# A half step of four rows of 256 tokens on 128 partitions in place of two rows of 480 on 64, in a fused attention and feed-forward kernel

## The chip, the cores and the metric

The kernel runs on one core of one Trainium2 chip. The metric is the device time of one execution in microseconds. The core has a matrix engine (PE, with its weight loads shown apart as PEld), a vector engine (DVE), an activation engine (ACT), a general engine (POOL) and a sync engine (SP), which here issues every transfer between the chip's main memory and the on-chip memory of 128 partitions. Each engine works through its own instructions in program order and waits on semaphores for the others.

## What is computed

Four batches of 12,480 tokens with 128 channels are reduced to 32 summary rows each by attention (the 32 `inducing` rows ask, all tokens answer), and then every token attends to the 32 rows of its batch. The result goes through a feed-forward network of 2,048 units with the nonlinearity h - tanh(h).

```python
B, N, m, C = 4, 12480, 32, 128
scale = 1.0 / np.sqrt(C)
def mab(q, kv):
    s = scale * (q @ kv.transpose(0, 2, 1))
    s = s - s.max(-1, keepdims=True)
    a = np.exp(s)
    a /= a.sum(-1, keepdims=True) + 1e-09
    return a @ kv
h = mab(I, x)                      # I: inducing, for each batch
x = mab(x, h).reshape(B * N, C)    # every token over 32 rows
g = x @ w_in                       # 128 -> 2048
return (g - np.tanh(g)) @ w_out    # 2048 -> 128
```

## The kernel before

The kernel never forms the 2,048 units of each token. A token's attention result is a weighted mean of the 32 rows of its batch, so the feed-forward network is expanded around the mean of those rows: `linear` makes one 32x128 matrix per batch (kept four times over the partitions as `P4`), which takes a token's 32 attention weights to its output. A bound (`bound`) is computed beside it; if it were exceeded, a general path behind a branch would run. On these inputs it does not.

A batch is cut into steps of 1,920 tokens (`SG`): four rows (`NQ`) of 480 tokens (`SEG`), one row for each group of 32 partitions, so that a step's scores for 32 queries fill 128 partitions by 480. 12,480 tokens are six such steps and a half step of 960 tokens. In the kernel before, the half step has two rows of 480 and fills 64 partitions. `SGS` lists the steps.

The first half of a batch (`first`, which calls `attend` for one or two groups of steps): for each step, SP loads `xT` (channels on partitions, L347); PE makes the scores against the 32 inducing rows (L332) into a bank of PSUM; DVE copies them to `s1` and takes the maximum (L358). When a group's maximum is known (`nb`), ACT takes the exponential (L408), DVE transposes blocks of 32x32 (`et`, L412), and PE sums the weighted tokens into `bank` (L419), 15 column steps of 32 tokens per row. For that it needs the tokens on partitions (`xn`): either SP loads them from a second copy in memory (L401, `in_xn`, or `in_xl` for the half step), or, for the steps listed in `TURNED`, PE transposes `xT` (L391) and ACT copies the result (L397). From the sums comes the batch's `hT` (L478 on PE, L480 on DVE), and from that `linear`.

The second half (`second`, `b_chain`): PE makes each step's scores against `hT` (L332 again), DVE transposes (`be`, L604) and takes maxima (L606), POOL subtracts (L611), ACT takes the exponential (L613), POOL folds 32 columns to 16 (L618), DVE sums and inverts (L621, L624), POOL scales (L625), DVE transposes back (`bt`, L628), PE multiplies by `P4` (`o`, L653), ACT copies `o` out of PSUM to `ot` (L659; in the last batch DVE may take it too, and the target is a free `xT` buffer), and SP stores it (L663). Stores hold 960 tokens each.

The two weight matrices arrive as 64-bit floats and are taken apart to 32-bit on DVE, ACT and POOL (`weight`, L283 to L308), through buffers of the `xn` pool.

The order is planned while the program is built. Every piece of work is entered with `add`: engine, planned cost, buffers read and written, a priority. `Plan.order` plays the plan through: whenever an engine is free it starts the ready piece with the lowest priority number, provided that the pools still have buffers (`PLACES`, for example ten `xT`, five `xn`, six `ot`, three PSUM banks `ps`). The numbers of `ORD` shift the priorities by batch and kind. The instructions are then issued in that order, on each engine's queue, and stay in it. Where the plan sees PE idle, matmuls on `ident` without use are put in (L744), in the share `FILL` of the gap.

```python
SGS = [(s * SG, NQ) for s in range(NS)] + ([(NS * SG, QL)] if QL else [])
...
add("SP", nq * 0.6, lambda x=x, s=s, P=P: nc.sync.dma_start(
    out=x.get()[:P], in_=xn[b, :, s * KB:(s + 1) * KB, :] if s < NS else xl[b]),
...
for _ in range(int(FILL * gaps.get(op, 0.0) / 0.25)):
    nc.tensor.matmul(bank[:, 2 * C:2 * C + 128], lhsT=ident, rhs=ident, start=first_fill, stop=True,
```

Of the kernel before, what the change touches and what calls it, by code (L numbers as in the profile page):

```python
# [30 lines left out]
ORD = dict(first=(-155, 195, 380, 915), second=(430, 815, 820, 935), fs=(16, 24, 10, 6), ss=(56, 54, 79, 44),  # L31
           lx=(-251, -205, -237, -234), ln=(-61, -146, -54, -80), lns=(8, 1, 49, 8), turn=(59, 65, 77, 55),
           keep=(-35, -146, -86, -29), q=(-534, -529, -468, -487), half=(-225, -211, -158, -86),
           late=(220, 276, 264, 244), guard=1420, win=-237, wout=-113, lwin=-162.5, lwout=291.5,
           store=(-272, -267, -265, -343), base=(43, 109, 36, 51))
# [150 lines left out]
def fused_kernel(ctx, tc, xT, xn, xl, indT, w_in, w_out, outT):  # L186
    nc = tc.nc
    C, NTOK = xT.shape
    B = xn.shape[0]
    m = indT.shape[1]  # L190
# [4 lines left out]
    QL = (N - NS * SG) // SEG  # L195
    SGS = [(s * SG, NQ) for s in range(NS)] + ([(NS * SG, QL)] if QL else [])
# [132 lines left out]
    def scores(ps, rows, w):  # L329

        for q, row in enumerate(rows):
            nc.tensor.matmul(ps[q * m:(q + 1) * m, :SEG], lhsT=w, rhs=row, start=True, stop=True)  # L332

    def attend(b, pri, s1, group, nbs, sms, at, hacc):
# [9 lines left out]
        for s in group:  # L344
            base, nq = SGS[s]
            x = xT_b[b, s] = io_buf("xT", [C, SG])
            add("SP", nq * 0.6, lambda x=x, base=base, nq=nq: nc.sync.dma_start(  # L347
                out=x.get()[:, :nq * SEG], in_=xT[:, b * N + base:b * N + base + nq * SEG]),
                writes=[x], pri=pri + s - of("lx", b), lag=IN_LAG, turn="xT")
            ps = misc()  # L350

            def pe(x=x, ps=ps, nq=nq):
                t = x.get()[:, :nq * SEG].rearrange("c (k q j) -> c k q j", k=KB, j=32)
                scores(ps.get(), [t[:, :, q, :] for q in range(nq)], indT_sb)
            add("PE", 0.96, pe, reads=[x, ind_b, s1], writes=[ps], pri=pri + of("fs", b) * s)
# [4 lines left out]
            add("DVE", 0.68, out, reads=[ps, s1], writes=[s1_part[s], mxg], pri=pri + of("fs", b) * s)  # L360
# [18 lines left out]
        for s in group:  # L379
            base, nq = SGS[s]  # L380
            P = nq * m
            x = io_buf("xn", [128, KB, C])
            parts = []
            if (b, s) in TURNED and nq == NQ:
                for k in range(0, KB, NT):
                    n = min(NT, KB - k)
# [13 lines left out]
            else:  # L400
                add("SP", nq * 0.6, lambda x=x, s=s, P=P: nc.sync.dma_start(  # L401
                    out=x.get()[:P], in_=xn[b, :, s * KB:(s + 1) * KB, :] if s < NS else xl[b]),
                    writes=[x], pri=p + of("lns", b) * s - of("ln", b), lag=IN_LAG, turn="xn")
            q0 = p + of("q", b) + of("fs", b) * s

            def ex(s=s, P=P):
                sl = s1.get()[:P, s, :]
                nc.scalar.activation(out=sl, in_=sl, func=AF.Exp, scale=SC, bias=nb.get()[:P],  # L408
                                     accum_out=sums.get()[:P, s:s + 1])
            add("ACT", 0.88, ex, reads=[nb, s1], writes=[s1_part[s], sums], pri=q0)  # L410
            et = io_buf("et", [128, KB, m])
            add("DVE", 0.66, lambda et=et, s=s, P=P: nc.vector.transpose(  # L412
                out=et.get()[:P].rearrange("p k i -> p (k i)"), in_=s1.get()[:P, s, :]),
                reads=[s1_part[s], s1], writes=[et], pri=q0)

            def acc(et=et, x=x, s=s, P=P):
                for k in range(KB):
                    q = k % NQ
                    nc.tensor.matmul(hacc.get()[q * m:(q + 1) * m, :], lhsT=et.get()[:P, k, :], rhs=x.get()[:P, k, :],  # L419
                                     start=(s == group[0] and k < NQ), stop=(s == group[-1] and k >= KB - NQ))  # L420
            last = add("PE", 1.03, acc, reads=[et, x, *parts], writes=[hacc], pri=q0)
# [166 lines left out]
    def b_chain(b, nq, x, xs, pri, S, out, roomy):  # L588
        P = nq * m
        ps = misc()  # L590
        add("PE", 0.96, lambda: scores(ps.get(), [xs()[:, q * SEG:(q + 1) * SEG] for q in range(nq)], hTs[b]),
# [12 lines left out]
        add("DVE", 0.68, lambda: nc.vector.transpose(out=be.get()[:P].rearrange("p k i -> p (k i)"), in_=ps.get()[:P, :SEG]),  # L604
            reads=[ps, *held], writes=[be], pri=pri)
        add("DVE", 0.64, lambda: nc.vector.tensor_reduce(out=bmx.get()[:P], in_=be.get()[:P], axis=AX.X, op=ALU.max),  # L606
            reads=[be], writes=[bmx], pri=pri)

        def wide(t):
            return t.unsqueeze(2).to_broadcast([P, KB, m])  # L610
        add("POOL", 1.02, lambda: nc.gpsimd.tensor_tensor(out=be.get()[:P], in0=be.get()[:P], in1=wide(bmx.get()[:P]), op=ALU.subtract),  # L611
            reads=[bmx], writes=[be], pri=pri)
        add("ACT", 0.6, lambda: nc.scalar.activation(out=be.get()[:P], in_=be.get()[:P], func=AF.Exp, scale=SC),  # L613
# [4 lines left out]
        add("POOL", 0.7, lambda: nc.gpsimd.tensor_tensor(out=bs.get()[:P, :, :m // 2], in0=be.get()[:P, :, :m // 2],  # L618
                                                         in1=be.get()[:P, :, m // 2:], op=ALU.add),
            reads=[be], writes=[bs], pri=pri)  # L620
        add("DVE", 0.42, lambda: nc.vector.tensor_reduce(out=S()[:P], in_=bs.get()[:P], axis=AX.X, op=ALU.add),  # L621
            reads=[bs], writes=[part], pri=pri)
        s_parts.append(part)
        add("DVE", 0.24, lambda: nc.vector.reciprocal(out=brs.get()[:P], in_=S()[:P]), reads=[part], writes=[brs], pri=pri)  # L624
        add("POOL", 1.02, lambda: nc.gpsimd.tensor_tensor(out=be.get()[:P], in0=be.get()[:P], in1=wide(brs.get()[:P]), op=ALU.mult),  # L625
            reads=[brs], writes=[be], pri=pri)

        add("DVE", 0.67, lambda: nc.vector.transpose(out=bt.get()[:P], in_=be.get()[:P].rearrange("p k i -> p (k i)")),  # L628
# [3 lines left out]
    def second(b, s, pri):  # L632
        base, nq = SGS[s]
        x = xT_b[b, s]
        n = (b * NSG + s) * KB

        def out(bt, held):
            ots = []
            for h in range(nq // 2):
                if b < B - 1:  # L640
                    ots.append(io_buf("ot", [128, 2 * SEG]))
                else:
                    if h == 0:

                        wide = io_buf("xT", [C, SG])
                    ots.append(Buf(lambda wide=wide, h=h: wide.get()[:, 2 * h * SEG:2 * (h + 1) * SEG]))
            keep = [wide] if b == B - 1 else []
            tiles = [Buf(lambda: ps_o.tile([128, 2, 512], F32, name="o"), "o") for _ in range(nq // 2)]

            def pe(qs):  # L650
                for q in qs:
                    p = slice(q * m, (q + 1) * m)
                    nc.tensor.matmul(tiles[q // 2].get()[:, q % 2, :SEG], lhsT=P4_b[b].get()[p, :], rhs=bt.get()[p, :],  # L653
                                     start=True, stop=True)

            add("PE", 1.05, lambda: pe(range(nq)), reads=[bt, *held, P4_b[b]], writes=tiles, pri=pri)
            for h, (o, ot) in enumerate(zip(tiles, ots)):
                def ev(copy, o=o, ot=ot):
                    copy(out=ot.get().rearrange("p (q n) -> p q n", q=2), in_=o.get()[:, :, :SEG])  # L659
                add("ACT", 0.97, lambda ev=ev: ev(nc.scalar.copy), reads=[o, *keep], writes=[ot], pri=pri,  # L660
                    other=("DVE", 1.14, lambda ev=ev: ev(nc.vector.tensor_copy), pri + 1000) if b == B - 1 else None)
                at = b * N + base + 2 * h * SEG
                add("SP", 1.2, lambda ot=ot, at=at: nc.sync.dma_start(out=outT[:, at:at + 2 * SEG], in_=ot.get()),  # L663
                    reads=[ot, *keep], pri=pri - of("store", b), lag=OUT_LAG)
        b_chain(b, nq, x, x.get, pri, lambda: sums_all.get()[:, n:n + KB], out, b == B - 1 and s % 2 == 1)


# [190 lines left out]
```

## Time and profile before

| | us |
|---|---|
| Three runs, median (lowest to highest) | 216.4 (213.31 to 217.84) |
| Profiled execution | 213.38 |
| Its span, first to last instruction | 211.8 |
| PE busy in it | 177.3 |
| DVE busy | 150.5 |
| ACT busy | 118.1 |
| POOL busy | 96.6 |

The profile is of one execution. Busy times overlap; a stage is limited by whatever ends last in it. The page cuts the span into 40 slices of 5.3 us and gives the busy tenths of each engine, the PE clock that was granted, the share of time in which the 16 transfer engines had packets, and the rate in GB/s. The lines that carry the argument stand in the prediction.

### The profile page before, as it was taken

How to read it: one execution, taken by the hardware profiler on the slowest of the kernel's cores; microseconds unless marked ns; L12 is line 12 of the kernel's file. 1: busy time of each engine (PE TensorE's matmuls, PEld its weight loads, DVE VectorE, ACT ScalarE, POOL GpSimd, SP SyncE). 2: the span in 40 equal slices, each digit the busy share in tenths (PEclk: the TensorE clock that was granted, in tenths of full speed). 3: DMA queues.
4: the chain of work that ended last, by engine and by line, in shares of the span. 5: the costliest groups of instructions: out<-in, count | busy, mean ns of one | idle time of the engine just before them, and what ended most of it. 6: DMA issues, size and time to landing. Idle time of an engine off the chain costs nothing.

```text
span 211.8 us, 5313 instructions
## 1 busy us (share of the span) xinstructions
PE 177.3 (84%) x2055; PEld 96.6 (46%) x2055; DVE 150.5 (71%) x392; ACT 118.1 (56%) x230; POOL 96.6 (46%) x138
## 2 busy tenths in 40 slices
PE   7589988489897896999699499986999699899950
PEld 7544566353352365542225366431556334346620
DVE  5798469519997975479679637896688227997970
ACT  2446658313323876577549457553997456566530
POOL 1044003201599543148846306597427224989610
PEclk9969999958999999999999979999999959999995
DMA  5999999999799999999999999999999991548791
GB/s 169 414 425 422 406 387 373 199 410 371 245 413 429 361 351 292 424 405 422 425 409 400 345 367 395 356 331 376 429 403 310 408 415 73 204 161 354 305 398 75
DMA packets 15468, 73.40 MB, mean 346 GB/s; under 512 B 1872, under 2 KB 1872, under 8 KB 15440
## 3 DMA queue, kind: packets, MB, share of 16 engines
q1 hardware_dynamic: 15440, 73.03, 90.2%
q8 instruction: 17, 0.28, 0.5%
q14 instruction: 11, 0.09, 0.1%
HBM read 47.46 MB, written 25.56 MB: 345 GB/s over the span
## 4 chain that ended last, share of the span: by engine, by line
PE 41%; DMA 38%; DVE 7%; ACT 5%; issue 3%; SPq 2%; POOL 1%; ACTq 0%; DVEq 0%; POOLq 0%
DMA xT<-in_xT 22%; PE ps_m L332 11%; PE o L653 10%; PE bank L419 5%; PE ps_m L391 5%; DMA xn<-in_xl 5%; PE bank L744 4%; DMA xn<-in_xn 4%; DMA xn<-in_w_out 4%; DMA outT<-ot 4%; PE ps_m L501 2%; ACT ot L659 2%; PE ps_m L513 2%; ACT s L408 1%; PE ps_m L459 1%
## 5 line engine op out<-in xcount | busy, mean ns | idle before, releaser
L659 ACT COPY ot<-o 128x960 f32<-128x960 f32 x39 | 36.5, 957 | 13.2 <-PE o L653 7.2
L419 PE MATMUL bank<-xn,et 128*32 128x128 f32 (+1 forms) x840 | 32.0, 285 | 7.7 <-DMA xn<-in_xn 3.4
L332 PE MATMUL ps_m<-xT,indT_sb 128*32 128x480 f32 x208 | 29.9, 625 | 9.4 <-DMA xT<-in_xT 7.3
L611 POOL TENSOR_TENSOR be<-be,bmx 128x480 f32<-128x480 f32 (+1 forms) x25 | 25.6, 1028 | 17.6 <-DVE bmx L606 16.5
L625 POOL TENSOR_TENSOR be<-be,brs 128x480 f32<-128x480 f32 (+1 forms) x25 | 24.7, 993 | 17.3 <-DVE brs L624 12.5
L419 PEld LDWEIGHTS bank<-xn,et 128*32 128x32 f32 (+1 forms) x840 | 24.9, 113 | 15.4 <-issue 6.0
L653 PE MATMUL o<-bt,P 32*128 32x480 f32 x184 | 29.6, 623 | 1.1 <-ACT ot L659 1.0
L332 PE MATMUL ps_m<-xT,hT_all 128*32 128x480 f32 x208 | 27.4, 586 | 0.7 <-DVE be L604 0.5
L618 POOL TENSOR_TENSOR bs<-be 128x240 f32<-128x240 f32 (+1 forms) x25 | 17.4, 697 | 22.3 <-ACT be L613 17.7
L397 ACT COPY xn<-ps_m 128x512 f32<-128x512 f32 (+1 forms) x32 | 17.1, 560 | 16.1 <-PE ps_m L391 16.1
L358 DVE TENSOR_SCALAR_CACHE_REDUCE s<-ps_m 128x480 f32<-128x480 f32 (+1 forms) x28 | 18.1, 645 | 10.3 <-PE ps_m L332 10.2
L744 PE MATMUL bank<-ident 128*128 128x128 f32 x150 | 23.3, 303 | 1.4 <-POOL ident masks.py:199 1.4
L744 PEld LDWEIGHTS bank<-ident 128*128 128x128 f32 x150 | 20.4, 211 | 6.2 <-issue 4.8
L391 PE MATMUL ps_m<-ident,xT 128*128 128x128 f32 x120 | 18.8, 299 | 4.3 <-DMA xT<-in_xT 3.7
L408 ACT ACTIVATE s<-s,nb 128x480 f32<-128x480 f32 (+1 forms) x28 | 19.5, 697 | 3.2 <-DVE nb L377 3.2
L391 PEld LDWEIGHTS ps_m<-ident,xT 128*128 128x128 f32 x120 | 14.3, 151 | 12.9 <-issue 3.6
L613 ACT ACTIVATE be<-be 128x480 f32<-128x480 f32 (+1 forms) x25 | 14.9, 606 | 8.8 <-POOL be L611 8.8
L412 DVE STREAM_TRANSPOSE et<-s 128x480 f32<-128x480 f32 (+1 forms) x28 | 17.9, 651 | 2.5 <-ACT s L408 2.4
L308 POOL TENSOR_TENSOR wout_sb<-wout_sb,xn 128x512 f32<-128x512 f32 x4 | 5.6, 1398 | 30.5 <-DVE xn L304 26.6
L628 DVE STREAM_TRANSPOSE bt<-be 128x480 f32<-128x480 f32 (+1 forms) x25 | 16.4, 657 | 4.0 <-POOL be L625 3.8
L604 DVE STREAM_TRANSPOSE be<-ps_m 128x480 f32<-128x480 f32 (+1 forms) x25 | 16.3, 660 | 3.8 <-PE ps_m L332 3.8
L606 DVE TENSOR_REDUCE bmx<-be 128x15 f32<-128x480 f32 (+1 forms) x25 | 15.5, 621 | 0.1
(126 smaller groups left out, 223.6 us busy)
## 6 DMA issues: line engine op xcount, KB each, us to landing
xT<-in_xT SPq DMA_DIRECT2D x24, 960.0 KB, 8.8
outT<-ot SPq DMA_DIRECT2D x39, 480.0 KB, 8.2
xn<-in_xn SPq DMA_DIRECT2D x16, 960.0 KB, 9.4
outT<-xT SPq DMA_DIRECT2D x13, 480.0 KB, 2.9
xn<-in_w_in SPq DMA_DIRECT2D x4, 512.0 KB, 5.4
xn<-in_w_out SPq DMA_DIRECT2D x4, 512.0 KB, 8.4
xT<-in_xT SPq DMA_DIRECT2D x4, 480.0 KB, 8.8
xn<-in_xl SPq DMA_DIRECT2D x4, 480.0 KB, 9.1
```

The source lines that it names most:

```text
L332: nc.tensor.matmul(ps[q * m:(q + 1) * m, :SEG], lhsT=w, rhs=row, start=True, stop=True)
L358: nc.vector.tensor_scalar(out=s1.get()[:P, s, :], in0=ps.get()[:P, :SEG], scalar1=1.0, scalar2=None, op0=ALU.mult, op1=ALU.max, accum_out= ...
L391: nc.tensor.transpose(out=pt.get()[:, i * 128:(i + 1) * 128], in_=xT_b[b, s].get()[:, (k + i) * 128:(k + i + 1) * 128], identity=ident)
L408: nc.scalar.activation(out=sl, in_=sl, func=AF.Exp, scale=SC, bias=nb.get()[:P], accum_out=sums.get()[:P, s:s + 1])
L412: add("DVE", 0.66, lambda et=et, s=s, P=P: nc.vector.transpose(out=et.get()[:P].rearrange("p k i -> p (k i)"), in_=s1.get()[:P, s, :]), re ...
L419: nc.tensor.matmul(hacc.get()[q * m:(q + 1) * m, :], lhsT=et.get()[:P, k, :], rhs=x.get()[:P, k, :], start=(s == group[0] and k < NQ), sto ...
L611: add("POOL", 1.02, lambda: nc.gpsimd.tensor_tensor(out=be.get()[:P], in0=be.get()[:P], in1=wide(bmx.get()[:P]), op=ALU.subtract), reads=[ ...
L618: add("POOL", 0.7, lambda: nc.gpsimd.tensor_tensor(out=bs.get()[:P, :, :m // 2], in0=be.get()[:P, :, :m // 2], in1=be.get()[:P, :, m // 2: ...
L625: add("POOL", 1.02, lambda: nc.gpsimd.tensor_tensor(out=be.get()[:P], in0=be.get()[:P], in1=wide(brs.get()[:P]), op=ALU.mult), reads=[brs] ...
L653: nc.tensor.matmul(tiles[q // 2].get()[:, q % 2, :SEG], lhsT=P4_b[b].get()[p, :], rhs=bt.get()[p, :], start=True, stop=True)
L659: copy(out=ot.get().rearrange("p (q n) -> p q n", q=2), in_=o.get()[:, :, :SEG])
L744: nc.tensor.matmul(bank[:, 2 * C:2 * C + 128], lhsT=ident, rhs=ident, start=first_fill, stop=True, skip_group_check=not first_fill)
```

## The change

The half step is laid out as four rows of 256 tokens on 128 partitions (`HEG`), 1,024 tokens in all. A batch has only 960 left, so the half step begins 64 tokens (`DUP`) earlier and repeats the last 64 of the step before. In the first half of the attention the repeated tokens must not count twice: their scores (64 partitions by 32 columns) are set to -3.0e38 after the maximum is taken. In the second half their outputs are computed and not stored: the half step's two copies go side by side into one `ot` buffer, and one store takes the 960 tokens behind the repeated ones. The column steps of L419 become 8 for 15 in the half step, the loads of it 128 partitions by 4 KB for 64 by 7.5 KB (`xl`) and 4 KB for 3.75 KB a partition (`xT`).

Pools change (`xT` 11 for 10, `bt` 2 for 5, `et` 4 for 3, `ot` 5 for 6 and larger), `ORD`, `FILL` and the lag that the plan takes for loads (`IN_LAG`) get new numbers, and `TURNED` has nine steps for eight.

```diff
+HEG = 256
+HB = HEG // 32
+DUP = NQ * HEG - SG // 2
-FILL = 0.7
-PLACES = dict(xT=10, xn=5, s1=1, be=5, bt=5, et=3, ot=6, ps=3, o=2, bs=1, D=1, M4=1, P1=2, P4=2)
+FILL = 0.8
+PLACES = dict(xT=11, xn=5, s1=1, be=5, bt=2, et=4, ot=5, ps=3, o=2, bs=1, D=1, M4=1, P1=2, P4=2)
-ORD = dict(first=(-155, 195, 380, 915), second=(430, 815, 820, 935), fs=(16, 24, 10, 6), ss=(56, 54, 79, 44),
+ORD = dict(first=(-205, 200, 455, 875), second=(435, 945, 825, 1020), fs=(16, 32, 18, 9), ss=(21, 111, 96, 66),
...
-TURNED = {(0, 0), (0, 2), (0, 3), (0, 4), (2, 0), (2, 1), (3, 0), (3, 3)}
+TURNED = {(0, 0), (0, 1), (0, 2), (0, 3), (0, 5), (2, 0), (2, 4), (3, 0), (3, 5)}
-IN_LAG, OUT_LAG = 2.5, 1.7
+IN_LAG, OUT_LAG = 2, 1.7
...
-    SGS = [(s * SG, NQ) for s in range(NS)] + ([(NS * SG, QL)] if QL else [])
+    SGS = [(s * SG, SEG, 0) for s in range(NS)] + ([(NS * SG - DUP, HEG, DUP)] if N > NS * SG else [])
...
+    def share(us, seg):
+        return us if seg == SEG else 0.15 + (us - 0.15) * seg / SEG
...
-            def out(ps=ps, s=s, P=nq * m):
-                nc.vector.tensor_scalar(out=s1.get()[:P, s, :], in0=ps.get()[:P, :SEG], scalar1=1.0, scalar2=None,
-                                        op0=ALU.mult, op1=ALU.max, accum_out=mxg.get()[:P, s:s + 1])
+            def out(ps=ps, s=s, seg=seg, dup=dup):
+                nc.vector.tensor_scalar(out=s1.get()[:, s, :seg], in0=ps.get()[:, :seg], scalar1=1.0, scalar2=None,
+                                        op0=ALU.mult, op1=ALU.max, accum_out=mxg.get()[:, s:s + 1])
+                if dup:
+
+                    nc.vector.memset(s1.get()[:dup, s, :32], -3.0e38)
...
-                add("SP", nq * 0.6, lambda x=x, s=s, P=P: nc.sync.dma_start(
-                    out=x.get()[:P], in_=xn[b, :, s * KB:(s + 1) * KB, :] if s < NS else xl[b]),
+                add("SP", NQ * seg / 800.0, lambda x=x, s=s, kb=kb: nc.sync.dma_start(
+                    out=x.get()[:, :kb], in_=xn[b, :, s * KB:(s + 1) * KB, :] if s < NS else xl[b]),
...
+            elif full:
+                ots, keep = [io_buf("ot", [128, NQ * HEG]) for _ in range(2)], []
+            else:
+                whole = io_buf("ot", [128, NQ * HEG])
+                ots = [Buf(lambda h=h: whole.get()[:, 2 * h * seg:2 * (h + 1) * seg]) for h in range(2)]
+                keep = [whole]
...
+            if not full:
+                at = b * N + base
+                add("SP", 1.2, lambda: nc.sync.dma_start(out=outT[:, at + dup:at + NQ * seg], in_=whole.get()[:, dup:NQ * seg]),
+                    reads=[whole, *ots], pri=pri - of("store", b), lag=OUT_LAG)
```

What this moves is shown at three places. The first is SP's queue from batch 0's loads to the first loads `xn` of batch 1. `xT` and `xn` are the token loads, `in_xl` the half step's rows, `in_w_out` the second weight matrix. Before:

```order
L347 DMA xT<-in_xT 128x1920 x6
L401 DMA xn<-in_xn 128x1920
L347 DMA xT<-in_xT 128x960
L283 DMA xn<-in_w_out 128x1024
L347 DMA xT<-in_xT 128x1920
L283 DMA xn<-in_w_out 128x1024
L347 DMA xT<-in_xT 128x1920
L401 DMA xn<-in_xn 128x1920
L401 DMA xn<-in_xl 64x1920
L347 DMA xT<-in_xT 128x1920
L283 DMA xn<-in_w_out 128x1024 x2
L401 DMA xn<-in_xn 128x1920 x4
```

Now, on the same queue:

```order
L354 DMA xT<-in_xT 128x1920 x6
L354 DMA xT<-in_xT 128x1024
L287 DMA xn<-in_w_out 128x1024 x2
L354 DMA xT<-in_xT 128x1920 x2
L411 DMA xn<-in_xn 128x1920
L287 DMA xn<-in_w_out 128x1024
L354 DMA xT<-in_xT 128x1920 x2
L411 DMA xn<-in_xl 128x1024
L287 DMA xn<-in_w_out 128x1024
L411 DMA xn<-in_xn 128x1920 x4
```

Batch 0 loads one `xn` where it loaded two, four loads `xT` of batch 1 stand ahead of the wait for free buffers where three stood, and `xl` stands behind them on 128 partitions.

The second place is PE, from the last batch's sums (`bank`) to its `linear` (`win_sb`). `P_1287` and `P_1826` are the matrices `P4` of batches 1 and 2, `fold,P` makes `hT`. Before:

```order
L653 MATMUL o<-bt,P_1287 128x480 x4
L419 MATMUL bank<-xn,et 32x128 x15
L459 MATMUL ps_m<-sm,fold 128x1
L419 MATMUL bank<-xn,et 32x128 x15
L653 MATMUL o<-bt,P_1826 128x480 x4
L478 MATMUL ps_m<-fold,P_2154 128x32
L744 MATMUL bank<-ident 128x128 x2
L501 MATMUL ps_m<-win_sb,hT_all 32x512 x4
```

Now, with `P_1857` for batch 2:

```order
L667 MATMUL o<-bt,P_1857 128x480 x4
L428 MATMUL bank<-xn,et 32x128 x15
L763 MATMUL bank<-ident 128x128
L428 MATMUL bank<-xn,et 32x128 x30
L468 MATMUL ps_m<-sm,fold 128x1
L667 MATMUL o<-bt,P_1857 128x480 x4
L428 MATMUL bank<-xn,et 32x128 x8
L763 MATMUL bank<-ident 128x128 x2
L487 MATMUL ps_m<-fold,P_2164 128x32
L667 MATMUL o<-bt,P_1857 128x480 x4
L510 MATMUL ps_m<-win_sb,hT_all 32x512 x4
```

An output matmul of batch 2 still stands ahead of the matmul for `hT`, now ahead of the half step's sums too, and fillers stand between.

The third place is PE in the tail, from the second scores of the last batch to its first output. `P_2326` is batch 3's matrix. Before:

```order
L653 MATMUL o<-bt,P_1826 128x480 x4
L332 MATMUL ps_m<-xT,hT_all 32x480 x12
L653 MATMUL o<-bt,P_1826 128x480 x2
L555 MATMUL ps_m<-wout_sb,M_2189 32x128 x16
L332 MATMUL ps_m<-xT,hT_all 32x480 x4
L559 MATMUL ps_m<-P_2306,fold 128x128
L332 MATMUL ps_m<-xT,hT_all 32x480 x2
L653 MATMUL o<-bt,P_2326 128x480 x4
```

Now, where `P_1239` is batch 1's matrix and `P_2347` batch 3's:

```order
L667 MATMUL o<-bt,P_1857 128x480 x4
L339 MATMUL ps_m<-xT,hT_all 32x480 x12
L763 MATMUL bank<-ident 128x128 x2
L564 MATMUL ps_m<-wout_sb,M_2201 32x128 x16
L667 MATMUL o<-bt,P_1857 128x256 x4
L568 MATMUL ps_m<-P_2323,fold 128x128
L339 MATMUL ps_m<-xT,hT_all 32x480 x4
L667 MATMUL o<-bt,P_1239 128x256 x4
L339 MATMUL ps_m<-xT,hT_all 32x256 x4
L701 MATMUL ps_m<-xT,cols 32x128 x16
L667 MATMUL o<-bt,P_2347 128x480 x4
```

The outputs of the half steps of batches 1 and 2 stand here now, and the half step's scores and the matmul of the bound have moved up among them. In all, fillers on `ident` go from 75 to 88 instructions, and the turned steps' transposes from 120 to 135.

More of the change, by code (lines that the diff above doesn't have):

```diff
@@ L422, in attend @@
+            last = add("PE", share(1.03, seg), acc, reads=[et, x, *parts], writes=[hacc], pri=q0)
         p += of("fs", b) * NSG + of("half", b)
@@ L586, in fused_kernel, with b_chain @@
     s_parts = []
[L588 to L589 removed]
+    def b_chain(b, seg, x, xs, pri, S, out, roomy):
+        kb = seg // 32
         ps = misc()
[L591 removed]
+        add("PE", share(0.96, seg), lambda: scores(ps.get(), [xs()[:, q * seg:(q + 1) * seg] for q in range(NQ)], hTs[b], seg),
             reads=[x, hT_b[b]], writes=[ps], pri=pri)
@@ L657, in out @@
             for h, (o, ot) in enumerate(zip(tiles, ots)):
                 def ev(copy, o=o, ot=ot):
[L659 to L664, printed above, removed]
@@ L665, in second @@
-        b_chain(b, nq, x, x.get, pri, lambda: sums_all.get()[:, n:n + KB], out, b == B - 1 and s % 2 == 1)
+                    copy(out=ot.get()[:, :2 * seg].rearrange("p (q n) -> p q n", q=2), in_=o.get()[:, :, :seg])
+                add("ACT", share(0.97, seg), lambda ev=ev: ev(nc.scalar.copy), reads=[o, *keep], writes=[ot], pri=pri,
+                    other=("DVE", share(1.14, seg), lambda ev=ev: ev(nc.vector.tensor_copy), pri + 1000) if b == B - 1 else None)
+                if full:
+                    at = b * N + base + 2 * h * seg
+                    add("SP", 1.2, lambda ot=ot, at=at: nc.sync.dma_start(out=outT[:, at:at + 2 * seg], in_=ot.get()[:, :2 * seg]),
+                        reads=[ot, *keep], pri=pri - of("store", b), lag=OUT_LAG)
@@ L829 @@
     NS = N // SG
-    QL = (N - NS * SG) // SEG
     def words(a):
```

115 lines of the change are left out of this document (56 added, 59 removed).

## The prediction

> **What bounds the kernel now.** I read the page's slices and queues first, then the chain, then windows of the two stages. In the slices the reader sees the transfers running at about 410 GB/s nearly throughout, with hollows, and a last fifth with little traffic; the queue's packets fill 90% of the span.
>
> ```profile
> PEclk9969999958999999999999979999999959999995
> GB/s 169 414 425 422 406 387 373 199 410 371 245 413 429 361 351 292 424 405 422 425 409 400 345 367 395 356 331 376 429 403 310 408 415 73 204 161 354 305 398 75
> q1 hardware_dynamic: 15440, 73.03, 90.2%
> PE 41%; DMA 38%; DVE 7%; ACT 5%; issue 3%; SPq 2%; POOL 1%; ACTq 0%; DVEq 0%; POOLq 0%
> ```
>
> Windows (length, busy time of PE, weight loads, DVE, ACT, POOL, then the PE clock, DMA share and rate) split the span in two stages:
>
> ```profile
> 0.00:168.00 168.00, 142.02 (x1787) 79.40 (x1789) 122.87 (x327) 95.94 (x195) 73.93 (x105) 0.96 0.98 371
> 168.00:207.00 39.00, 35.31 (x270) 17.17 (x266) 27.64 (x65) 22.14 (x36) 22.67 (x33) 0.90 0.70 280
> ```
>
> To 168 us the transfers are the limit (share 0.98; the fullest engine, PE, is busy 142 of 168, filler matmuls among it). Behind it the last batch's second half is a chain through all engines. A microsecond of transfer taken from the first stage should come off the end; in the second stage only the chain counts.
>
> The next view is decisive: the four loads of a half step's rows (64 partitions) as SP issued them, and windows at the hollows, each with a full one beside it.
>
> ```profile
> 33.28 0.56 SPq L401 DMA_DIRECT2D xn<-in_xl  x1
> 76.64 0.47 SPq L401 DMA_DIRECT2D xn<-in_xl  x1
> 116.06 0.48 SPq L401 DMA_DIRECT2D xn<-in_xl  x1
> 158.37 0.47 SPq L401 DMA_DIRECT2D xn<-in_xl  x1
> ...
> 31.00:36.00 5.00, 4.32 (x81) 3.51 (x71) 4.79 (x15) 3.22 (x6) 1.14 (x1) 1.00 1.02 409
> 36.50:42.00 5.50, 2.42 (x63) 1.72 (x61) 3.51 (x14) 2.26 (x7) 1.29 (x2) 1.00 0.98 187
> 42.50:47.00 4.50, 3.87 (x42) 2.82 (x46) 0.61 (x3) 0.18 (x1) 0.00 (x0) 0.50 1.03 415
> 81.00:83.00 2.00, 1.14 (x28) 0.75 (x20) 1.92 (x7) 2.00 (x7) 0.54 (x1) 1.00 0.96 173
> 85.00:90.00 5.00, 5.00 (x68) 2.71 (x66) 2.32 (x10) 2.72 (x5) 0.70 (x1) 1.00 1.03 424
> 121.00:123.00 2.00, 2.00 (x16) 1.66 (x19) 0.00 (x0) 0.94 (x3) 0.49 (x1) 0.50 0.99 246
> 126.00:131.00 5.00, 5.00 (x89) 3.44 (x81) 3.10 (x11) 3.83 (x8) 2.64 (x3) 1.00 1.01 419
> 161.00:164.00 3.00, 2.55 (x61) 1.61 (x57) 2.24 (x7) 2.08 (x5) 1.93 (x3) 1.00 0.93 262
> 165.00:170.00 5.00, 3.33 (x38) 1.60 (x38) 1.38 (x5) 3.15 (x4) 1.65 (x2) 0.87 1.02 413
> ```
>
> Some 3 to 5 us after each issue the rate falls to between 173 and 262 GB/s while the engines' share stays at 0.93 to 0.99: busy, at about half speed.
>
> **The change, part by part.** (a) The half step's rows go to 128 partitions. What each hollow lost, in time at its neighbour's rate: 5.5 x (1 - 187/409) = 3.0 us, 2.0 x (1 - 173/424) = 1.2, 2.0 x (1 - 246/419) = 0.8, 3.0 x (1 - 262/413) = 1.1. The last three are alike, 1.05 on the mean. The first moved 5.5 x 0.187 = 1.03 MB, twice a half load, so something besides may be in it. I count it like the others: 4 x 1.05 = 4.2 us gained; 6.2 with all of it is one end, 0 (the hollows come from something else) the other.
>
> [...]
>
> (b) Bytes. Loads by kind:
>
> ```profile
> outT<-ot SPq DMA_DIRECT2D x39, 480.0 KB, 8.2
> xn<-in_xn SPq DMA_DIRECT2D x16, 960.0 KB, 9.4
> xn<-in_xl SPq DMA_DIRECT2D x4, 480.0 KB, 9.1
> ```
>
> Steps turned on PE go from eight to nine, so 16 loads xn become 15: -0.98 MB. The 64 repeated tokens add 32 KB to four loads xl and four xT: +0.26 MB. Net -0.72 MB, at 415 GB/s 1.7 us gained. Stores keep number and bytes.
>
> (c) Work of the half steps. The rows are the 64-partition forms, their neighbours, and rows between which 128x256 lies (busy us, mean ns):
>
> ```profile
> L412 DVE STREAM_TRANSPOSE et<-s 64x480 f32<-64x480 f32 x4 | 2.6, 638 | 0.4 <-ACT s L408 0.4
> L439 DVE COPY hA<-bank 128x128 f32<-128x128 f32 x3 | 0.9, 289 | 5.9 <-PE bank L419 5.9
> L611 POOL TENSOR_TENSOR be<-be,bmx 64x480 f32<-64x480 f32 x4 | 4.0, 988 | 1.0 <-DVE nbm L449 1.0
> L618 POOL TENSOR_TENSOR bs<-be 64x240 f32<-64x240 f32 x4 | 2.8, 691 | 4.7 <-ACT be L613 2.9 <-DVE S_all L621 1.8
> L517 ACT COPY D<-ps_m 128x256 f32<-128x256 f32 x8 | 2.9, 371 | 0.7 <-DVE mean L518 0.7
> L397 ACT COPY xn<-ps_m 128x512 f32<-128x512 f32 x24 | 13.8, 588 | 16.1 <-PE ps_m L391 16.1
> L659 ACT COPY ot<-o 128x960 f32<-128x960 f32 x39 | 36.5, 957 | 13.2 <-PE o L653 7.2 <-PE bank L419 3.6 <-DMA outT<-ot 2.2
> L391 PE MATMUL ps_m<-ident,xT 128*128 128x128 f32 x120 | 18.8, 299 | 4.3 <-DMA xT<-in_xT 3.7
> L419 PE MATMUL bank<-xn,et 64*32 64x128 f32 x120 | 5.1, 308 | 2.6 <-DMA xn<-in_xl 2.6
> L659 DVE COPY xT<-o 128x960 f32<-128x960 f32 x4 | 4.6, 1143 | 0.8 <-PE o L653 0.8
> L653 PE MATMUL o<-bt,P 32*128 32x480 f32 x184 | 29.6, 623 | 1.1 <-ACT ot L659 1.0
> ```
>
> DVE: 638 ns at 480 and 289 at 128 elements give 416 at 256, so five passes save 1.1 us a half step, less a small memset: about 4 us in all. POOL: between 0.53 (in proportion) and 0.71 us (the line through 240 and 480 elements) for 0.99; I take 0.62, which with the sum saves 0.9 a half step. ACT: two copies of 512 (1.18) for one of 960 (0.96) cost 0.2, the two exponentials save about as much each. PE: eight column steps for fifteen save 28 of the 60 at L419 (5.1/60 each): 2.4 us. The ninth turned step costs PE 15 x 18.8/120 = 2.4 us and ACT 3 x 0.59 + 0.48 = 2.2. Fillers go from 75 to 88, only where PE is to wait. In the first stage all this lies under the transfers, which leave PE 26 us of room: 0. If PE were the limit there, the turned step and the fillers would cost 2.4 us and some 4.
>
> (d) The tail, from the last batch's copy hT to the limit:
>
> ```profile
> 171.39 0.19 DVE L480 COPY hT_all<-ps_m 128x32 f32<-128x32 f32 x1 [0.92 <-PE ps_m L478]
> 206.35 0.14 DVE L721 TENSOR_SCALAR limit<-low 1x1 f32<-1x1 f32 x1
> ```
>
> It is 35.1 us long. POOL saves 0.9 and DVE 1.1 in the last half step, but DVE takes six evictions of the last batch for four (one of half size, 1.14 + 0.6 = 1.7 more), and on PE one more full step of batch 2 and the half step of batch 1 stand there (29.6/184 is 0.16 a record, eight records a step: 1.3 and 0.65). The chain runs through POOL and DVE more than PE; I take 0, ends -2 and +2.
>
> (e) The new order. In SP's queue batch 0's rows stand behind two more loads xT but no longer slowed; one more xT buffer lets a fourth load of batch 1 start early. A hole remains where loads wait for weight staging and scores:
>
> ```profile
> 52.00:56.00 4.00, 3.39 (x30) 2.15 (x30) 3.94 (x11) 2.31 (x8) 1.66 (x2) 1.00 0.52 156
> ```
>
> 4 x (1 - 156/415) = 2.5 us. Nearly the same bytes stand ahead of it (ten loads xT and six xn before, eleven and five now, with xl and all the weights), so I leave it: 0, ends -2.5 and +2.5.
>
> Sum: -4.2 - 1.7 = -5.9 us. The profiled execution took 213.38 us (span 211.8, 1.6 around it); it becomes 207.5. That execution lies near the lowest of the three runs (213.31) and 3.0 below their median of 216.4; from the median the sum gives 210.5. I forecast between the two, 209.0.
>
> **Rivals.** First, the hollows have another cause than the 64 partitions and stay. Then only the bytes count: 213.4 - 1.7 = 211.7, at the median 214.7, no change. For it speaks the overlong first hollow; against it that every hollow follows a half load.
>
> Second, on the other side, the store buffers `ot` fall from six to five. One is held for its copy and landing, 0.96 + 8.2 = 9.2 us. Thirteen stores of a batch through six take at least 13/6 x 9.2 = 19.9 us, through five 23.9: 4.0 more. PE is in order, and an output matmul stands ahead of the last batch's L478, where one wait of this kind is seen already:
>
> ```profile
> 167.67 3.12 PE L653 MATMUL o<-bt,P 32*128 32x480 f32 x8 [1.04 <-ACT ot L659]
> 167.81 0.96 ACT L659 COPY ot<-o 128x960 f32<-128x960 f32 x1 [0.19 <-DMA outT<-ot]
> ```
>
> If all three batches pay it, 12.0 - 5.9 = +6.1: 219.5. It decides from 5.9 us of such waits on, one and a half batches' worth. Against it: ACT waited 2.2 us in all for stores with six (the row of L659 above).
>
> Third, the tail's clock. After PE's idle time around 166 us (2.4 busy of 4.1) it ran at half clock just where the last batch's `linear` begins:
>
> ```profile
> 164.50:168.60 4.10, 2.44 (x41) 1.40 (x36) 1.41 (x5) 1.75 (x2) 0.99 (x1) 1.00 1.02 412
> 168.60:175.30 6.70, 6.62 (x28) 2.65 (x30) 1.42 (x4) 4.42 (x7) 1.68 (x2) 0.51 1.00 409
> ```
>
> At full clock its 6.6 us of matmuls would take 3.4, at most 3.2 less than the forecast's sum: 204.3. Fillers stand closer to that place now, but PE still waits there for xl. [...]
>
> **How the numbers follow.** Forecast 0.60 (its own range 203 to 212: 6.2 gained and the tail's 2 at one end, the median's 210.5 and some loss in the tail at the other); hollows stay 0.20; stores 0.12; clock 0.08. The range 203 to 215.5 leaves out the store rival's 219.5 and a little below. A measurement of this kernel tells about 2% from no change, 4.3 us: faster is forecast and clock, 0.68; same is the hollows and a mild store case, 0.22; slower the rest, 0.10.
>
> **What would show it.** In the profile after: loads xl on 128 partitions, and windows 3 to 5 us behind their issue at 400 GB/s and more (a); 15 loads xn and 72.3 MB in the queue (b); the end of heavy traffic, 175 us before, some 6 us earlier; the tail from the last batch's L480 copy to the limit as long as before (d). Wrong it would be if that traffic ends early but the tail starts no earlier, or if ACT's waits for landing stores reach several microseconds.

## The result, and the profile after

| | us |
|---|---|
| Before, median of six runs (lowest to highest) | 214.49 (212.9 to 217.84) |
| After, median of six runs | 205.29 (201.55 to 207.19) |
| Ratio, with 95% interval | 0.9464 (0.9362 to 0.9565) |
| After, measured again (six runs), beside its own runs of before | 205.21; before 213.41 |
| Ratio of that second measurement | 0.9634 (0.9572 to 0.9696) |
| Profiled execution after | 204.65, span 202.9 |

The kernel became faster: by 5.4% in the first measurement, by 3.7% in the second; by medians 9.2 and 8.2 us. The medians count every execution, the ratios only the faster of the two groups into which the executions of a kernel fall by clock and time, so the two differ by some microseconds. The forecast was 209.0 us, 7.4 below the median of 216.4 then known, and its sum 5.9. The direction was right and the time lies in the range of 203 to 215.5, but the gain was put too low.

The page of the changed kernel, slices of 5.1 us, the queue, and the shares of the chain that ended last (DMA was 38% of it, now 41%):

```profile
PEclk9969999999999999699999999999997599999996
GB/s 180 400 427 421 405 423 382 411 407 417 423 368 337 363 422 403 399 282 400 351 392 424 420 414 364 371 357 414 401 286 401 316 296 246 182 181 318 404 402 121
q1 hardware_dynamic: 15552, 72.31, 91.0%
DMA 41%; PE 39%; DVE 8%; ACT 3%; SPq 2%; issue 2%; POOL 0%; DVEq 0%; ACTq 0%
```

The bytes are the forecast's (72.3 MB), and the deepest hollow of the first stage's slices, 199 GB/s at 37 to 42 us, is gone. The heavy traffic ends at about 169.5 us where it ended at 175.5. Next come the four issues of xl after, and windows that begin some 3 us behind each (busy times, PE clock, DMA share, GB/s):

```profile
35.01 0.33 SPq L411 DMA_DIRECT2D xn<-in_xl  x1
60.72 0.33 SPq L411 DMA_DIRECT2D xn<-in_xl  x1
107.64 0.33 SPq L411 DMA_DIRECT2D xn<-in_xl  x1
150.39 1.03 SPq L411 DMA_DIRECT2D xn<-in_xl  x1
...
38.00:42.00 4.00, 3.40 (x53) 2.04 (x53) 3.23 (x15) 2.59 (x5) 0.09 (x1) 1.00 0.99 384
64.00:68.00 4.00, 3.99 (x43) 1.16 (x35) 3.83 (x14) 3.29 (x8) 2.65 (x4) 1.00 1.00 375
111.00:115.00 4.00, 3.27 (x30) 1.96 (x30) 3.93 (x14) 3.56 (x9) 2.41 (x3) 1.00 1.02 430
153.00:157.00 4.00, 2.72 (x56) 2.39 (x59) 0.53 (x3) 0.18 (x3) 0.99 (x1) 0.72 1.01 413
52.00:56.00 4.00, 2.20 (x44) 1.76 (x40) 3.82 (x8) 2.31 (x6) 2.66 (x6) 1.00 1.01 421
86.00:90.00 4.00, 4.00 (x64) 1.47 (x52) 3.19 (x8) 1.36 (x3) 0.86 (x4) 0.94 0.73 251
```

Where the rate was 173 to 262 it is 375 to 430 (the prediction had named 400 and more as the sign; two of the four stay a little below). The hole at 52 to 56 us (156 GB/s before) is closed as well; another one stands at 86 to 90. The stages follow from the copies of `hT`, one per batch, and from the last copy of outputs. Before (the prediction shows the fourth `hT`, at 171.39 us), and after:

```profile
50.55 0.19 DVE L480 COPY hT_all<-ps_m 128x32 f32<-128x32 f32 x1
90.56 0.18 DVE L480 COPY hT_all<-ps_m 128x32 f32<-128x32 f32 x1
131.49 0.15 DVE L480 COPY hT_all<-ps_m 128x32 f32<-128x32 f32 x1
...
204.06 1.16 DVE L659 COPY xT<-o 128x960 f32<-128x960 f32 x1 [0.80 <-PE o L653]
```

```profile
44.83 0.19 DVE L489 COPY hT_all<-ps_m 128x32 f32<-128x32 f32 x1
76.00 0.19 DVE L489 COPY hT_all<-ps_m 128x32 f32<-128x32 f32 x1
122.07 0.19 DVE L489 COPY hT_all<-ps_m 128x32 f32<-128x32 f32 x1 [0.27 <-PE ps_m L487]
163.72 0.19 DVE L489 COPY hT_all<-ps_m 128x32 f32<-128x32 f32 x1 [0.84 <-PE ps_m L487]
...
193.49 0.14 DVE L740 TENSOR_SCALAR limit<-low 1x1 f32<-1x1 f32 x1
193.57 1.16 DVE L673 COPY xT<-o 128x960 f32<-128x960 f32 x1
195.38 0.69 DVE L673 COPY xT<-o 128x512 f32<-128x512 f32 x1 [0.66 <-PE o L667]
```

The last output was copied by 205.2 us before and by 196.1 after. So of the 8.9 us by which the span shrank (211.8 to 202.9) the first stage gives 7.7, and the tail from `hT` to the last output 1.4 (33.8 us to 32.4); behind the last output 0.2 are lost. The prediction's own measure of the tail, up to the `limit` instruction, went from 35.1 to 29.9 us, but only because that instruction now stands ahead of the last two copies.

Batch 1 is 14.6 us ahead and gives half of it back. SP's queue shows both: 14 loads xT, 7 loads xn and no store stand in front of its xl, where 17, 8 and 1 stood, and the loads that it went ahead of come later: between the xl of batch 1 and that of batch 2 there are ten loads xT for five.

### The profile page after: what moved, and what is told of

Its sections match the earlier page's. It is cut to its first block, busy times and chain, and to the rows that moved or that the text cites. A ratio compares the mean times of both kernels' runs of the same rounds, so it can differ in the third digit from the quotient of the medians.

```text
span 202.9 us, 5388 instructions
## 1 busy us (share of the span) xinstructions
PE 172.1 (85%) x2088; PEld 98.8 (49%) x2088; DVE 149.3 (74%) x398; ACT 117.3 (58%) x236; POOL 91.1 (45%) x138
## 3 DMA queue, kind: packets, MB, share of 16 engines
q1 hardware_dynamic: 15552, 72.31, 91.0%
## 4 chain that ended last, share of the span: by engine, by line
DMA 41%; PE 39%; DVE 8%; ACT 3%; SPq 2%; issue 2%; POOL 0%; DVEq 0%; ACTq 0%
DMA xT<-in_xT 29%; PE ps_m L339 12%; PE bank L428 8%; PE o L667 8%; DMA outT<-ot 5%; DMA xn<-in_xn 4%; DMA xn<-in_xl 4%; PE ps_m L401 3%; PE bank L763 3%; DVE xT L673 2%; PE ps_m L510 1%; DVE xn L302 1%; PE ps_m L522 1%; SPq L287 1%; ACT xn L407 1%
## 5 line engine op out<-in xcount | busy, mean ns | idle before, releaser
L673 ACT COPY ot<-o 128x960 f32<-128x960 f32 (+1 forms) x42 | 37.1, 910 | 19.9 <-PE o L667 10.2
L339 PE MATMUL ps_m<-xT,indT_sb 128*32 128x480 f32 (+1 forms) x224 | 28.8, 586 | 11.3 <-DMA xT<-in_xT 10.8
L428 PE MATMUL bank<-xn,et 128*32 128x128 f32 x784 | 29.8, 286 | 4.0 <-DMA xn<-in_xn 3.2
L620 POOL TENSOR_TENSOR be<-be,bmx 128x480 f32<-128x480 f32 (+1 forms) x25 | 23.8, 952 | 16.7 <-DVE bmx L615 15.4
L428 PEld LDWEIGHTS bank<-xn,et 128*32 128x32 f32 x784 | 24.0, 114 | 13.5 <-issue 4.1
L667 PE MATMUL o<-bt,P 32*128 32x480 f32 (+1 forms) x200 | 28.5, 600 | 0.5 <-ACT ot L673 0.4
L763 PE MATMUL bank<-ident 128*128 128x128 f32 x176 | 26.8, 297 | 1.8 <-POOL ident masks.py:199 1.3
L763 PEld LDWEIGHTS bank<-ident 128*128 128x128 f32 x176 | 23.0, 203 | 8.3 <-issue 5.7
L407 ACT COPY xn<-ps_m 128x512 f32<-128x512 f32 (+1 forms) x36 | 19.1, 565 | 13.3 <-PE ps_m L401 13.1
L339 PE MATMUL ps_m<-xT,hT_all 128*32 128x480 f32 (+1 forms) x224 | 25.1, 545 | 0.6 <-ACT D L526 0.4
```

What stands on the lines that cost most here:

```text
L339: nc.tensor.matmul(ps[q * m:(q + 1) * m, :seg], lhsT=w, rhs=row, start=True, stop=True)
L407: nc.scalar.copy(out=x.get()[:, k:k + n, :].rearrange("p k c -> p (k c)"), in_=pt.get()[:, :n * 128])
L620: add("POOL", share(1.02, seg), lambda: nc.gpsimd.tensor_tensor(out=be.get()[:, :kb], in0=be.get()[:, :kb], in1=wide(bmx.get()[:, :kb]), o ...
L667: nc.tensor.matmul(tiles[q // 2].get()[:, q % 2, :seg], lhsT=P4_b[b].get()[p, :], rhs=bt.get()[p, :seg], start=True, stop=True)
L673: copy(out=ot.get()[:, :2 * seg].rearrange("p (q n) -> p q n", q=2), in_=o.get()[:, :, :seg])
```

## The experiments

The theory at this point: the half loads on 64 partitions were slow and the layout cures that (P). Its rival: the new order, pools and turned steps bring the gain (O).

### Layout alone, order alone

The first kernel is the changed one with the old `ORD`, `PLACES`, `TURNED`, `FILL` and `IN_LAG`:

```diff
-FILL = 0.8
-PLACES = dict(xT=11, xn=5, s1=1, be=5, bt=2, et=4, ot=5, ...
+FILL = 0.7
+PLACES = dict(xT=10, xn=5, s1=1, be=5, bt=5, et=3, ot=6, ...
...
-IN_LAG, OUT_LAG = 2, 1.7
+IN_LAG, OUT_LAG = 2.5, 1.7
```

> The new layout with all the old numbers (order, pools, turned steps, lag, fillers). Theory P (the half loads on 64 partitions were slow, and the layout cures it): no hollow behind the four loads xl, 5 to 6 us less than before, 208 to 210 us. Theory O (the new order and pools bring the gain): 213 to 215 us, even if the hollows are gone.

Measured: 225.96 us against 214.07 for before, ratio 1.0587 (1.0512 to 1.0662). It is slower than before and after, and neither theory had it. SP's queue shows the place:

```profile
152.83 0.34 SPq L354 DMA_DIRECT2D xT<-in_xT  x1
153.26 19.47 SPq L678 DMA_DIRECT2D outT<-ot  x9
174.48 0.34 SPq L411 DMA_DIRECT2D xn<-in_xn  x1
175.35 0.34 SPq L411 DMA_DIRECT2D xn<-in_xl  x1
```

The last batch's last two loads stand behind nine stores and are issued at 174.5 and 175.4 us, where the kernel before issued them at 156.7 and 158.4. The planner takes other costs for the half steps of the new layout, and the old priorities then come out as another order. `hT` of the last batch comes at 184.4 us. The numbers of `ORD` belong to one layout; this run says nothing of the layout's own worth.

The second kernel is the old one with all the new numbers, the same diff the other way round.

> The old layout with all the new numbers. Theory P: the hollows of 1 to 3 us behind each load xl are still there; only the one load xn less is gained, 2.4 us, 211 to 213 us. Theory O: 205 to 207 us, as with the whole change.

Measured: 215.7 us (212.56 to 218.36), against 214.07 (208.09 to 219.36) for before on the same chip; there is no ratio for it. The new order alone shows no gain, with 0.98 MB less to load. Its windows behind xl (issued at 35.7, 62.0, 114.4 and 166.3 us):

```profile
40.00:47.00 7.00, 3.30 (x51) 1.80 (x50) 3.14 (x12) 1.75 (x4) 1.26 (x1) 1.00 1.02 260
66.00:71.00 5.00, 5.00 (x35) 1.24 (x35) 4.20 (x14) 2.93 (x4) 4.11 (x6) 1.00 1.03 277
122.00:128.00 6.00, 3.81 (x28) 0.92 (x20) 1.67 (x5) 1.66 (x3) 2.29 (x3) 0.92 1.01 195
168.00:171.00 3.00, 3.00 (x60) 2.77 (x51) 1.01 (x4) 1.49 (x2) 0.99 (x1) 0.50 0.95 247
```

The hollows are back, and three of them are longer than the kernel before had them (2 to 3 us in its batches 1 to 3). On SP's queue the three long ones have loads behind their xl (a load of w_out, then xn; two loads xT; one load xT, issued at 119.1 us), the short one has eleven stores. So what follows xl in the queue seems to matter.

### The partitions, everything else held

Two kernels from the changed one. Order, work and bytes are the same; each load xl becomes two loads, once by partitions, once by columns.

```diff
+                    for p in (slice(0, 64), slice(64, 128)):
+                        nc.sync.dma_start(out=x.get()[p, :kb], in_=xl[b, p])
```

> The changed kernel, each load xl issued as two loads of 64 partitions, everything else the same. Theory P: 512 KB at half rate again, a hollow of about 2.3 us at about 200 GB/s behind each, 4 to 5 us more than the changed kernel: 209 to 211 us. Rival (the hollows came from something else, such as what stood beside xl in the queue): rates above 400 GB/s, 205 to 206 us.

```diff
+                    for k in (slice(0, 4), slice(4, 8)):
+                        nc.sync.dma_start(out=x.get()[:, k], in_=xl[b, :, k])
```

> The changed kernel, each load xl issued as two loads of 128 partitions by half the columns: the control of the two halves, with the same number of issues on SP. Both theories: no hollow, 205 to 206 us. If it is as slow as the two halves, the cost there is the second issue and not the partitions.

Measured: 212.19 us by partitions, ratio to before 0.9893 (0.9834 to 0.9951); 205.11 by columns, 0.9607 (0.9546 to 0.9667). The second issue costs nothing that shows (the changed kernel took 205.29 and 205.21); the partitions cost 7.1 us by medians, 6.1 by the ratios (0.0286 of 214). The window behind batch 0's xl, first by partitions, then by columns:

```profile
41.00:47.00 6.00, 2.22 (x46) 1.10 (x39) 2.80 (x9) 1.04 (x3) 1.26 (x1) 0.89 1.04 241
```

```profile
41.00:47.00 6.00, 5.01 (x84) 2.64 (x80) 4.55 (x15) 1.68 (x4) 1.28 (x1) 1.00 1.03 410
```

Theory P holds, at a price above the 4 to 5 us expected. Measured is 1.5 to 1.8 us for each of the four loads.

The same from the other side: the kernel before, untouched but for its four loads xl, which bring their bytes to 128 partitions.

```diff
+                        nc.sync.dma_start(out=x.get().rearrange("p k c -> p (k c)")[:, :960], in_=xl[b])
```

> The kernel before with its order, its pools and its work untouched; only the four loads xl bring the same bytes to 128 partitions (960 elements each) instead of 64. The sums of the half steps then use wrong rows of the tokens, at the same cost. If the price of the 64 partitions in this order is what I counted in the prediction (1.05 us each), 4 us less than before: 210 us. If it is what the two halves cost in the changed kernel (212.2 against 205.1 us, 7 us), 207 to 208 us. If the old order cannot use the time (rival), within 1 us of before.

Measured: 209.35 us against 214.35 for before, 5.0 less by medians; the ratio of 0.9847 makes it 3.3, with an interval from 0.9679 to 1.0014 that just takes in no change. The four loads xl are now issued up to 2.6 us earlier (33.5, 74.0, 114.4 and 156.7 us), so the windows of the later three are moved by as much:

```profile
36.50:42.00 5.50, 4.29 (x102) 3.43 (x105) 3.68 (x14) 2.48 (x7) 1.46 (x2) 1.00 1.01 403
78.50:80.50 2.00, 1.03 (x24) 0.64 (x16) 2.00 (x9) 2.00 (x6) 0.42 (x1) 1.00 1.00 403
119.50:121.50 2.00, 2.00 (x33) 0.84 (x26) 1.32 (x4) 0.27 (x1) 0.31 (x1) 1.00 0.99 403
159.50:162.50 3.00, 3.00 (x71) 1.90 (x64) 2.26 (x6) 1.95 (x4) 1.81 (x3) 1.00 0.78 307
```

The first three hollows are filled. In the last the rate is 307 at a share of 0.78, where it was 262 at 0.93: there the transfer engines now stand idle for a part of the time. So the whole of the first hollow belonged to the 64 partitions (3.0 us of loss by the prediction's reckoning): batch 0 is ready 3.5 us earlier (`hT` at 47.05 for 50.55), and the last batch 4.0 (167.44 for 171.39).

The hole at 52 to 56 us does not go with it. Over the 15 us around it, before, with wide loads alone, and in the changed kernel:

```profile
42.00:57.00 15.00, 13.26 (x108) 6.99 (x112) 9.87 (x25) 4.64 (x12) 2.66 (x3) 0.77 0.88 341
42.00:57.00 15.00, 11.59 (x97) 4.84 (x90) 13.00 (x31) 4.90 (x13) 5.42 (x9) 1.00 0.95 337
42.00:57.00 15.00, 11.68 (x143) 5.73 (x142) 13.15 (x31) 6.43 (x18) 7.75 (x16) 1.00 1.02 419
```

With wide loads in the old order it is shallower and longer, and as many bytes are missing as before; in the changed kernel it is closed.

### The load by itself

Four kernels that compute nothing: a stream of loads (or of stores) of 128 partitions, with a load of 0.524 MB between, 16 times, once on 64 partitions and once on 128.

```python
for i in range(16):
    step(2 * i)                                            # a load 128x1920, or two stores 128x960
    nc.sync.dma_start(out=hs[i % 4][:PARTS, :kb], in_=xl[i % 4])
    step(2 * i + 1)
```

> A stream of loads alone, no other work: 16 times a load of 128x1920, one of 64 partitions by 8 KB (0.524 MB), a load of 128x1920. If only its own bytes run at half rate, each small load costs 1.2 to 1.3 us more than on 128 partitions, 20 us in all, and the whole takes about 120 us. If it also slows the load that follows it, as the long hollow of batch 0 suggests, 2.5 us each, 40 us in all, about 140 us.

> The same stream of loads with the small one on 128 partitions by 4 KB, the same bytes (2.49 MB a round). Both theories: 415 GB/s throughout, 6.0 us a round, about 100 us in all. It is the base of the loads on 64 partitions.

> The small load of 64 partitions in a stream of stores: 16 times two stores of 128x960, the load, two stores. If only its own bytes are slow, the same 1.2 to 1.3 us each over 128 partitions as among loads. If the slowing goes over to what follows only for loads, about 1 us each here and 2.5 us among loads.

> The same stream of stores with the small load on 128 partitions: the base of the run before. About 400 GB/s, 6.2 us a round, some 105 us in all.

| one execution each, the first on another chip, us | 64 partitions | 128 partitions | each small load costs more by |
|---|---|---|---|
| among loads | 150.72 | 105.98 | 44.74 / 16 = 2.80 |
| among stores | 126.95 | 120.76 | 6.19 / 16 = 0.39 |

By the rates in the middle of the streams (292 for 419 GB/s among loads, 384 for 414 among stores, 2.49 MB a round) the small load costs 2.6 and 0.5 us more. Among loads that is the 2.5 of the theory that the neighbour is slowed too; the stream of stores was slower than expected with either load. The stream of loads with 64 partitions alternates between 5 us at half rate and 3 at full rate; below it stands the middle of the stream with 128 partitions (columns: length, busy POOL, PE clock, DMA share, GB/s):

```profile
46.00:51.00 5.00, 0.00 (x0) 1.00 1.00 234
51.00:54.00 3.00, 0.00 (x0) 1.00 1.02 408
54.00:59.00 5.00, 0.00 (x0) 1.00 1.04 241
```

```profile
20.00:90.00 70.00, 0.00 (x0) 1.00 1.02 419
```

In one hollow 5 x 0.234 = 1.17 MB move, the 0.524 of the small load and a little more than as much again of a 128-partition load beside it. Whether that is the load ahead or the one behind, the stream can't tell; the whole kernel speaks for the one behind. Before, a load xn stands directly ahead of each of the four xl (at 31.7, 75.4, 114.9 and 156.7 us), and only the first xl, with loads directly behind it, has the long hollow (5.5 us for 2 to 3); the new order with narrow loads agrees. The rate in the hollow is 234 to 241 GB/s, where the stream with 128 partitions runs at 419. Among stores the long hollow is missing (some 2 us of each round at 208 to 360 GB/s between 40 and 80 us), and even less is lost than the load's own bytes at half rate would lose (an estimate, 0.524 MB at 419 GB/s: 1.25 us). Why a following load is held back, these runs don't show.

### The rest: bytes, fillers, the shorter work

The changed kernel with 2.95 MB less to load:

```diff
+                ld = 12 if s < NS else kb
...
+                    out=x.get()[:, :ld], in_=xn[b, :, s * KB:s * KB + ld, :] if s < NS else xl[b]),
```

> The changed kernel, its 15 loads xn cut from 15 blocks of tokens to 12; the sums use the first blocks again in place of the rest. 2.95 MB less, 7.1 us at 415 GB/s. If the transfers still bound the first stage, 198 to 199 us. If after the change the chain through the engines is the limit (rival), 203 us or more.

Measured: 200.5 us, 4.8 and 4.6 less than the changed kernel and its column twin, which ran on other chips; by the ratios to before (0.937 against 0.9464 and 0.9634) it is 2.0 to 5.6. A megabyte is worth some 1.6 us at the end by medians (0.7 to 1.9 by the ratios) and not the 2.4 of its transfer: the first stage is still in good part, no longer wholly, bound by transfers. `hT` of the last batch came at 158.3 for 163.7.

Fillers, by `FILL = 0.0` and `FILL = 1.1` for 0.8:

> The changed kernel without any of the 88 filler matmuls, the order otherwise the same. I counted the fillers at nothing, since they stand where PE waits. If so and the clock does not depend on them, 205 us. If they keep PE's clock up, the granted clock falls from 0.96 to below 0.9 and the time rises by 2 us or more, to 207 to 210 us. If PE is short of time (rival), 2 us less.

> The changed kernel with the share of fillers at 1.1 in place of 0.8 (129 fillers for 88). Without fillers it took 207.5 us at a granted clock of 0.92. If PE's clock still costs time, 204 us or less at a clock above 0.96. If the fillers now stand in PE's way, 206 us or more.

Measured: without fillers 207.51 us at a clock of 0.923; with 129 of them 205.78 at 0.985; with the 88 of the change 205.21 at 0.962. The last two ran on one chip, the first on another, so the worth of the fillers is known less well than its 2.3 us by medians: beside its own runs of before each, it is 1.4 by medians and 5.0 by the ratios. More of them raise the clock and win nothing. The loss without fillers lies in the tail. The last `hT` came at 163.5 us without them and at 164.0 with the 88, the last output was copied by 199.6 and 196.4. From 185 to 200 us, without and with:

```profile
185.00:200.00 15.00, 10.29 (x42) 3.28 (x42) 10.44 (x24) 4.94 (x7) 4.74 (x7) 0.50 0.76 304
185.00:200.00 15.00, 10.49 (x82) 6.47 (x81) 10.44 (x24) 4.96 (x7) 4.85 (x7) 0.93 0.92 361
```

Without fillers PE ran at half clock there (0.50 for 0.93).

Last, the new order with wide loads and the old layout of the half step's work, beside the changed kernel on the same chip:

> The new order and pools with the old layout of the half step's work, only the loads xl on 128 partitions by 960 elements (the half steps' sums use wrong rows of the tokens at the same cost). The same without the wide loads took 215.7 us. If the load's partitions are the price there as in the two halves (7 us) and the half step's shorter work is worth nothing, 208 to 209 us without the layout's fitted order, and 205 to 206 us if the layout adds nothing at all. If the shorter work of 128 partitions is what is still missing, 210 us or more.

> The changed kernel itself, as the base beside the two others on the same chip: 205 us, 4 to 5% less than before.

Measured: 208.0 us, ratio 0.9656 (0.9563 to 0.9748), against 205.21 and 0.9634. Over the same kernel with narrow loads (215.7, on another chip) the wide loads gain 7.7 us, or 7.0 when each is taken beside its own runs of before. From 42 to 57 us it moves 408 GB/s, so the new order with wide loads closes the hole without the new layout. What the layout adds beyond the load, shorter passes and the order fitted to them, is 2.8 us by medians and 0.2% (0.5 us) by the ratios, whose intervals overlap: at most a few microseconds, its size open.

## Why the prediction was right or wrong

**The sum.** It had 5.9 us from (a) and (b), with (c), (d) and (e) at nothing each. Measured were 8.2 to 9.2 by medians. The step that failed is to add the parts as if each had one price: (a) was read in the old order and carried to the new one, and the new order, the tail and the shorter work were put at nothing.

**(a), the hollows: right in kind, and right in size for the old order alone.** I counted 4 x 1.05 = 4.2 us, because three hollows were alike, and set the rest of the first aside as something else. (The three give 1.03 on the mean, and all four add to 6.1, not 6.2.) In the old order the four loads cost 3.3 to 5.0 us, not clear of no change, so 4.2 stands as far as that run can say. The rest of the first hollow was nothing else: with wide loads it vanished whole, though the hole behind it then lost as much as before. The three short hollows each had stores directly behind their xl, the first had loads. In the new order, which puts loads behind three of the four, the 64 partitions cost 6.1 to 7.1 (two halves) or 7.0 to 7.7 (wide loads). The error was to count a slow load by its own bytes, and not to see that its price hangs on what stands behind it (2.80 us a load among loads, 0.39 among stores).

**(b), the bytes: right.** 72.31 MB as worked out; at the measured 1.6 us a megabyte the 0.72 MB are worth 1.2 us, not 1.7.

**(c), the half step's work: durations right, and of little weight.** After, the rows read:

```profile
L620 POOL TENSOR_TENSOR be<-be,bmx 128x256 f32<-128x256 f32 x4 | 2.5, 616 | 0.6 <-DVE bmx L615 0.6
L421 DVE STREAM_TRANSPOSE et<-s 128x256 f32<-128x256 f32 x4 | 1.7, 418 | 0.1
L673 ACT COPY ot<-o 128x512 f32<-128x512 f32 x6 | 3.3, 606 | 0.3 <-PE o L667 0.3
```

616, 418 and 606 ns against 620, 416 and 590 expected. That it all lies under the transfers is nearly so: the last comparison leaves between half a microsecond and 2.8.

**Fillers, counted at nothing,** are worth 2.3 us by medians as a whole, in the tail, where PE's clock was 0.50 without them and 0.93 with the 88 (185 to 200 us); the step from 75 to 88 was not varied alone.

**(d), the tail:** 1.4 us shorter, inside the ends given. `linear` of the last batch ran at full clock (1.00 from 164.7 to 166.0 us):

```profile
164.72 1.06 PE L510 MATMUL ps_m<-win_sb,hT_all 128*32 128x512 f32 x8
```

Before, the half clock lay on it (0.51 from 168.6 to 175.3 us, the same eight matmuls in 1.94 us). That was the third rival; part of it came. After, the half clock lies some microseconds earlier, on the last sums (0.52 from 154.5 to 161.5 us). The half clock followed short pauses elsewhere too: before, PE was idle for 3.1 of the 5.5 us from 36.5 to 42.0, and when the clock halved at about 42.4 us (0.50 from 42.5 to 47.0), none of its pauses there had lasted longer than some 1.3 us.

**(e), the hole at 52 to 56 us: wrong at 0.** From 42 to 57 us the kernel before moved 341 GB/s, the changed one 419: by an estimate from these rates 15 x (1 - 341/415) = 2.7 us less lost, of which the new hole at 86 to 90 us takes back 4 x (1 - 251/415) = 1.6. I had treated it as a matter of bytes ahead of it. Wide loads alone did not close it (337), the new order with wide loads did (408). With the tail's 1.4 and the half to 2.8 us of the last comparison these are the places, as far as the runs show, where the 2.3 to 3.3 us lie that the sum missed; the three overlap, and how the rest divides among them stays open.

**The rivals.** Hollows with another cause: refuted. Store buffers: the waits came, but not their price:

```profile
ACT ot L673 <- DMA outT<-ot: 9.5, 7, 3.8
```

9.5 us in seven waits for 2.2 us in two before, past the 5.9 from which I had let it decide, and one of the signs that I had named against the forecast. What the rival needed was PE held by ACT, and that did not grow. The output matmuls (0.4 below, 1.0 before) and their weight loads (2.9 and 2.5) waited for `ot` copies 3.3 us in all, for 3.5 before:

```profile
L667 PE MATMUL o<-bt,P 32*128 32x480 f32 x168 | 25.5, 634 | 0.5 <-ACT ot L673 0.4
```

ACT, busy for 117 of 203 us, had idle time to take its waits, and their sum was the wrong measure. The number of `ot` buffers alone was not varied. The account in full, by medians, each kernel beside its own runs of before: the new order with narrow loads +1.6 (215.7 against 214.07; fewer bytes and probably dearer hollows), wide loads -7.0, the half step's shorter work with its fitted order -2.8: -8.2, as in the second measurement.

## What to carry to other kernels

A load to only half the partitions was priced here by what stood around it on the queue: 0.39 us for 0.524 MB among stores, 2.80 among loads. So a price read in one order does not carry over to another. Look at the rate, not the busy share, to find such places: in the kernel before the share stayed at 0.93 and more in the hollows, while the rate fell to 173 to 262 GB/s from 409 to 424 beside them. And a table of priorities fitted to one layout cannot be used to judge another: the same layout was 6% slower than before with the old table and 4 to 5% faster with the new one.

## What the runs showed of the hardware that was not expected

Among loads, a load of 0.524 MB on 64 partitions slowed a 128-partition load beside it: 5 us at 234 GB/s for 1.17 MB, 2.80 us lost where its own bytes at half rate would lose an estimated 1.25 (0.524 MB at 419 GB/s). The whole kernel speaks for the load behind it: the hollow of 5.5 us had loads behind xl, those of 2 to 3 us had stores. In a stream of stores the same load lost 0.39 us. More fillers brought PE's mean clock from 0.962 to 0.985 without any gain in time (205.21 and 205.78 us), while without fillers it fell to 0.50 over the last 15 us of the outputs.
